# Retention and two feed-forwards: weight tiles asked for after the retention, conversion with four VectorE operations, a buffer of its own for x2

## The chip, the cores and the metric

The kernel runs on one core of a Trainium2 chip. The metric is the device time of one execution in microseconds, the median of three runs. All five engines are used: TensorE (PE, with its weight loads as PEld), VectorE (DVE), ScalarE (ACT), GpSimd (POOL) for a small multiplication, and SyncE (SP), whose queue issues nearly all DMA transfers.

## The reference

```python
# q, k, v: (4, 8, 576, 64); x then (2304, 512)
scores = matmul(q, k^T) / sqrt(64)
ret = scores * gamma_h ** (i - j)      # for i >= j, else 0
x = matmul(ret, v)                     # to 2304 tokens x 512
h = x @ w_in                           # 512 -> 2048
g = where(h >= 1, h, where(h <= -1, 0, (h + 1) ** 2 / 4))
x = g @ w_out                          # 2048 -> 512
out = ((x @ w_a) * (x @ w_b)) @ w_out2 # 512 -> 1536 -> 512
```

The weights are float64; the kernel gets them as raw 64-bit words.

## The kernel before

**Tiling.** The 2304 tokens are cut into 6 blocks of 384 (TB) and 18 chunks of 128. Every factor is held as two float32r parts, high and low, and a product is three matmuls (the list HL).

**Retention.** There are 36 units: a chunk times a half of the heads. A unit is loaded to `u` (L215), its values are scaled on POOL (L223), it is split into two parts `z` by ACT and DVE (L228, L229), its scores are formed on PE (`s`), masked and split (L245 to L251, `retf`, `ret`), and multiplied with the values and with the running state (`po`, `pn`). The product times the query factors, a part of the constant `con`, is the unit's share of x (L303: `xf`; L308 and L309 write both parts to `x`). The L309 rows therefore count finished units. The constant comes in two transfers on ACT's queue: a small one with masks and key factors, a large one (128 x 2560) with the query factors.

**Feed-forwards.** Work is cut in steps of one block of tokens and one chunk of 128 hidden columns. Five groups of steps follow each other: groups 0, 1 and 2 hold the hidden chunks 0 to 5, 6 to 10 and 11 to 15 of the first feed-forward, groups 3 and 4 the two halves of the second. In each group all six blocks are walked, so partial sums of groups 0 and 1 are stored to memory (`y`, L398) and read back in group 2 (`yin`, L390), where y_out adds them to x2, the second feed-forward's x, and stores it (x2d, L406). A step is l1 (12 matmuls `ph`, 24 in groups 3 and 4), an activation (L356 to L362, or L412 to L415) and l2 (12 matmuls `acc`, 9 wide ones later). The l2 of a step follows the l1 of the next.

**Retention beside group 0.** Six units, the first block's, run ahead; during each step of group 0 one more unit follows, until all 36 are done at the end of block 4.

**Weights.** A tile of weights is 128 x 512 words of 64 bits. It is loaded to `raw` (three buffers, L118) and converted to float32 by two ACT and four or five DVE operations (convert, L128 to L137: the float64's words are put together with shifts and masks, and L130 raises small magnitudes to a floor), then split into two parts (L142 on ACT, L143 on DVE) in one of 18 buffers, and of 14 more once the retention's buffers are gone. The main loop asks for tiles by a credit of one half per step, and at once where one of the next three steps needs one.

**Order.** The code's order gives priorities, and a scheduler with a plan of times puts the instructions of each engine in their final order: work that is asked for later fills holes in that plan. Every engine, and SP's queue, then works through its own list in order.

**x.** Blocks of x are stored once (xd) and loaded again for groups 1 and 2 (fetch_x, L340), asked for in the third step of the block before. x, and x2 in group 2, are taken from one pool of two buffers.

Of the kernel before, what the change touches and what calls it, by code (L numbers as in the profile page):

```python
# [9 lines left out]
F32 = mybir.dt.float32  # L10
F32R = mybir.dt.float32r
# [3 lines left out]
AF = mybir.ActivationFunctionType  # L15
ALU = mybir.AluOpType
# [3 lines left out]
P = 128  # L20
TB = 384
CPB = TB // P
GROUPS1 = [(0, 6), (6, 11), (11, 16)]
GROUPS2 = [(0, 6), (6, 12)]
WBUFS, WBUFS2 = 18, 14
MID = 288
UW = 1280
Q0, K0, R0, V0 = 0, 512, 768, 1024
# [46 lines left out]
def retention_ffn_kernel(  # L75
# [12 lines left out]
    nc = tc.nc  # L88
    B, H, S, D = shape
    DM = H * D  # L90
    NCC = DM // P
    NB = B * S // TB
# [4 lines left out]
    xpool = ctx.enter_context(tc.tile_pool(name="x", bufs=2))  # L97
# [8 lines left out]
    def mm(o, l, r, start, stop):  # L106
        nc.tensor.matmul(o, l, r, start=start, stop=stop)  # L107
# [8 lines left out]
    def load_raw(src):  # L116
        raw = rpool.tile([P, 512], I64, tag="raw", name="raw")
        nc.sync.dma_start(raw.rearrange("p (c f) -> p c f", f=src.shape[-1]), src)  # L118
        return raw

    def convert(raw):

        w = raw.bitcast(U32).rearrange("p (n t) -> p t n", t=2)
        low, high = w[:, 0, :], w[:, 1, :]
        r = raw.bitcast(I32).rearrange("p (n t) -> p t n", t=2)[:, 0, :]
        t = cpool.tile([P, 512], F32, tag="conv", name="conv")
        tu, ti = t.bitcast(U32), t.bitcast(I32)
        nc.scalar.activation(t, high.bitcast(F32), AF.Abs, scale=2.0 ** 16)  # L128
        nc.scalar.activation(r, low, AF.Copy, scale=2.0 ** -29)  # L129
        nc.vector.tensor_scalar(out=t, in0=t, scalar1=2.0, scalar2=None, op0=ALU.max)  # L130
        nc.vector.tensor_scalar(
            out=tu, in0=tu, scalar1=3, scalar2=None, op0=ALU.logical_shift_left
        )
        nc.vector.scalar_tensor_tensor(  # L134
            out=tu, in0=high, scalar=0x80000000, in1=tu, op0=ALU.bitwise_and, op1=ALU.bitwise_or
        )
        nc.vector.tensor_tensor(out=ti, in0=ti, in1=r, op=ALU.add)  # L137
        return t
# [23 lines left out]
    def fetch_to(n):  # L162
        while begun[0] < min(n, len(stream)):
            raws[begun[0]] = load_raw(stream[begun[0]][1])
            begun[0] += 1

    def weights_to(n):

        while made[0] < min(n, len(stream)):
            free = [r for r in room if room[r][1] > 0]  # L170
            if not free:
                return
            i = made[0]
            fetch_to(i + 1)
            key = stream[i][0]
            home[key] = free[0]
            room[free[0]][1] -= 1
            weights[key] = split(convert(raws.pop(i)), room[free[0]][0])
            made[0] += 1
            fetch_to(i + 3)  # L180

    def used(key):

        del weights[key]
        room[home.pop(key)][1] += 1
# [8 lines left out]
    con = apool.tile([P, const.shape[1]], F32, name="con")  # L194
# [3 lines left out]
    state = [apool.tile([P, 2 * P], F32, name=f"state{d}") for d in range(2)]  # L198
# [13 lines left out]
    def load_unit(u):  # L212
        if u < NU:
            units[u] = upool.tile([P, UW], F32, tag="u", name="u")
            nc.sync.dma_start(units[u], qkv[u // 2, u % 2])  # L215
# [96 lines left out]
    loaded, ready, scored, done = [0], [0], [0], [0]  # L312
# [25 lines left out]
    def fetch_x(b, space):  # L338
        t = xpool.tile([P, 2, NCC, TB], F32R, tag="x", name="x")
        nc.sync.dma_start(t.bitcast(F32), space[b])  # L340
        return t


    def l1(x, w):
        ph = ps.tile([P, 512], F32, tag="ps", name="ph")
        ops = []
        for cc in range(NCC):
            ws = slice(cc * P, (cc + 1) * P)
            for a, z in HL:
                ops.append((ph[:, :TB], w[:, a, ws], x[:, z, cc, :]))  # L350
        return ph, [(o, l, r, i == 0, i == len(ops) - 1) for i, (o, l, r) in enumerate(ops)]
# [34 lines left out]
    def fetch_y(b):  # L386
        for m in range(NCC):
            for i in range(2):
                t = yin[b, m, i] = ypool[0].tile([P, TB], F32, tag="yin", name="yin")
                nc.sync.dma_start(t, yd[i][b][:, m, :])  # L390

    def y_out(i, b):
        x = xpool.tile([P, 2, NCC, TB], F32R, tag="x", name="x2") if i == 2 else None
        for m, y in enumerate(ys.pop((i, b))):
            if i < 2:
                t = tpool.tile([P, TB], F32, tag="t", name="yst")
                (nc.scalar.copy if m % 2 else nc.vector.tensor_copy)(t, y[:, :TB])
                nc.sync.dma_start(yd[i][b][:, m, :], t)  # L398
            else:
                t, other = yin.pop((b, m, 0)), yin.pop((b, m, 1))  # L400
                nc.vector.tensor_add(t, t, other)
                nc.vector.tensor_add(t, y[:, :TB], t)
                nc.scalar.copy(x[:, 0, m, :], t)
                nc.vector.tensor_sub(x[:, 1, m, :], t, x[:, 0, m, :].bitcast(F32))
        if i == 2:
            nc.sync.dma_start(x2d[b], x.bitcast(F32))  # L406
# [44 lines left out]

    load_unit(0)
    cuts = [0, 2 * P + places * H, const.shape[1]]
    for i in range(2):
        nc.scalar.dma_start(con[:, cuts[i]:cuts[i + 1]], const[:, cuts[i]:cuts[i + 1]])
    load_unit(1)
    loaded[0] = 2
    fetch_to(1)

    warm = wpool.tile([P, 2, 512], F32R, tag="w", name="warm")  # L460
    nc.vector.memset(warm.bitcast(F32), 0.0)
    wacc = acc.tile([P, 512], F32, tag="acc0", name="wacc")
    for _ in range(8):
        mm(wacc, warm[:, 0, 0:P], warm[:, 1, :], True, True)
# [2 lines left out]
    for i in range(UPB):  # L467
        rounds_to(i + 1)
        weights_to(i)

    ypool = [None]
    gs = {}
    prev, back = None, None
    steps = [
        (i, b, f, f == f0, f == f1 - 1)
        for i, (f0, f1) in enumerate(GROUPS1 + GROUPS2) for b in range(NB) for f in range(f0, f1)
    ]

    def needed(step):
        return place[("o" if step[0] < 3 else "p", step[2])] + 1  # L480

    def finish(step):
        (l2 if step[0] < 3 else l2_2)(step)

    credit = 0.0
    for s, step in enumerate(steps):
        i, b, f, first, last = step
        f0, f1 = (GROUPS1 + GROUPS2)[i]
        credit += 0.5
        ahead = max(needed(t) for t in steps[s:s + 3])  # L490
        if made[0] < ahead:
            weights_to(ahead)
            credit = 0.0
        elif credit >= 1.0:
            weights_to(made[0] + 1)
            credit = 0.0
        if first:
            if i == 0:
                x = xt[b]
            else:  # L500
                x = xt.pop((i, b)) if (i, b) in xt else fetch_x(b, xd if i < 3 else x2d)
        due = min(UPB * (b + 1) + -(-(f - f0 + 1) * UPB // (f1 - f0)), NU) if i == 0 else NU
        if i < 3:
            ph, ops = l1(x, weights["i", f])
            for half in (ops[:6], ops[6:]):
                for o in half:
                    mm(*o)
                with tc.high_priority(60):
                    rounds_to(min(done[0] + 1, due))
            assert done[0] == due  # L510
            if b == NB - 1:
                used(("i", f))
            gs[step] = act1(ph)
        else:
            pair = []
            for j, key in enumerate("ab"):
                ph, ops = l1(x, weights[key, f])
                for o in ops:
                    mm(*o)
                pair.append(ph)  # L520
                if b == NB - 1:
                    used((key, f))
                if j == 0 and prev:
                    finish(prev)
                    prev = None
            gs[step] = act2(*pair)
        if prev:
            finish(prev)
        prev = step
        if i == 0 and first:  # L530
            nc.sync.dma_start(xd[b], x.bitcast(F32))
        if i == 0 and done[0] == NU and ypool[0] is None:
            att.close()
            ypool[0] = ctx.enter_context(tc.tile_pool(name="y", bufs=8))
            room["wx"] = [ctx.enter_context(tc.tile_pool(name="wx", bufs=WBUFS2)), WBUFS2]
        if i == 2 and first:
            fetch_y(b)
        if i == 4 and first:
            fetch_o(b)
        if f == f0 + 2:  # L540
            ni, nb = (i, b + 1) if b + 1 < NB else (i + 1, 0)
            if 0 < ni < 5 and not (ni == 0):
                xt[ni, nb] = fetch_x(nb, xd if ni < 3 else x2d)
# [25 lines left out]
```

## Time and profile before

| | us |
|---|---|
| median of 3 runs | 1026.21 (1025.89 to 1026.53) |
| the profiled execution | 1028.9 |
| its span | 1027.1 |
| PE busy / PEld busy | 984.7 / 942.3 |
| DVE / ACT / POOL busy | 585.7 / 438.2 / 32.0 |

The span goes from the first to the last instruction; the profiled execution's own time is a little longer. Matmuls are pipelined, so a busy PE need not be PE at its peak; PEld, the weight loads, stands beside it. The granted clock is a share of TensorE's full 2.4 GHz; 0.5 is its lower level of 1.2 GHz.

### The profile page before, as it was taken

How to read it: one execution, taken by the hardware profiler on the slowest of the kernel's cores; microseconds unless marked ns; L12 is line 12 of the kernel's file. 1: busy time of each engine (PE TensorE's matmuls, PEld its weight loads, DVE VectorE, ACT ScalarE, POOL GpSimd, SP SyncE). 2: the span in 40 equal slices, each digit the busy share in tenths (PEclk: the TensorE clock that was granted, in tenths of full speed). 3: DMA queues.
4: the chain of work that ended last, by engine and by line, in shares of the span. 5: the costliest groups of instructions: out<-in, count | busy, mean ns of one | idle time of the engine just before them, and what ended most of it. 6: DMA issues, size and time to landing. Idle time of an engine off the chain costs nothing.

```text
span 1027.1 us, 14058 instructions
## 1 busy us (share of the span) xinstructions
PE 984.7 (96%) x5504; PEld 942.3 (92%) x5504; DVE 585.7 (57%) x1083; ACT 438.2 (43%) x831; POOL 32.0 (3%) x44
## 2 busy tenths in 40 slices
PE   5699898999999999998999999999999999999998
PEld 4588797999999999998999999999999999999997
DVE  5999999788778933689456424534324321222222
ACT  5566665566567643676545323323222211111111
POOL 1111101110000000000000000000000000000000
PEclk6589899999999999999999999999999999999999
DMA  7564647255066852568665632532221131131100
GB/s 282 170 201 147 231 133 252 101 172 179 29 257 232 277 190 93 168 203 292 222 230 185 245 106 79 185 113 69 106 93 49 66 123 59 65 123 62 41 32 31
DMA packets 57475, 151.30 MB, mean 147 GB/s; under 512 B 4672, under 2 KB 37568, under 8 KB 52672
## 3 DMA queue, kind: packets, MB, share of 16 engines
q1 hardware_dynamic: 57120, 148.92, 41.6%
q10 hardware_dynamic: 288, 1.48, 0.4%
q8 instruction: 43, 0.70, 0.3%
q14 instruction: 24, 0.20, 0.1%
HBM read 112.63 MB, written 37.75 MB: 146 GB/s over the span
## 4 chain that ended last, share of the span: by engine, by line
PE 69%; DVE 16%; DMA 9%; issue 2%; ACT 2%; DVEq 0%; POOL 0%; SPq 0%; ACTq 0%
PE ph L107 40%; PE acc L107 25%; PE po L107 2%; DVE z L229 2%; DVE conv L134 2%; DVE conv L137 2%; DMA x<-xd 2%; DMA raw<-in_moe_w_in 2%; DMA y<-yst 1%; DMA raw<-in_moe_w_out 1%; DVE xf L303 1%; DVE t L358 1%; PE s L107 1%; DMA raw<-in_moe_w_b 1%; DVE w L143 1%
## 5 line engine op out<-in xcount | busy, mean ns | idle before, releaser
L107 PE MATMUL ph<-x,w 128*128 128x384 f32 x2880 | 535.4, 338 | 6.9 <-DMA x<-xd 3.9
L107 PEld LDWEIGHTS ph<-x,w 128*128 128x128 f32 x2880 | 507.7, 189 | 15.5 <-DMA x<-xd 4.6
L107 PE MATMUL acc<-g,w 128*128 128x384 f32 x1152 | 218.7, 336 | 1.5 <-ACT g L361 0.8
L107 PEld LDWEIGHTS acc<-g,w 128*128 128x128 f32 x1152 | 200.6, 188 | 2.8 <-ACT g L361 1.7
L413 DVE TENSOR_TENSOR t<-ph,t 128x384 f32<-128x384 f32 x72 | 40.1, 557 | 218.5 <-PE ph L107 214.6
L107 PE MATMUL acc<-w,g 128*128 128x512 f32 x648 | 161.5, 393 | 0.0
L107 PEld LDWEIGHTS acc<-w,g 128*128 128x128 f32 x648 | 120.5, 188 | 21.9
L414 ACT CAST g<-t 128x384 fp32r<-128x384 f32 x72 | 37.0, 514 | 187.1 <-DVE t L413 187.0
L412 ACT COPY t<-ph 128x384 f32<-128x384 f32 x72 | 34.5, 479 | 114.3 <-PE ph L107 114.3
L358 DVE SCALAR_TENSOR_TENSOR t<-t,ph 128x384 f32<-128x384 f32 x96 | 52.5, 550 | 38.7 <-ACT t L357 38.2
L356 ACT ACTIVATE t<-ph 128x384 f32<-128x384 f32 x96 | 47.0, 489 | 56.9 <-PE ph L107 51.6
L361 ACT CAST g<-t 128x384 fp32r<-128x384 f32 x96 | 49.1, 511 | 51.5 <-PE acc L107 27.3
L362 DVE TENSOR_TENSOR g<-t,g 128x384 fp32r<-128x384 f32 x96 | 53.2, 555 | 27.2 <-ACT g L361 27.0
L129 ACT ACTIVATE raw<-raw 128x512 int32<-128x512 uint32 x68 | 46.2, 679 | 46.5 <-DMA raw<-in_moe_w_out 15.6
L107 PE MATMUL s<-z 128*128 128x256 f32 x216 | 45.5, 324 | 18.6 <-ACT z L228 11.7
L229 DVE TENSOR_TENSOR z<-u,z 128x1280 fp32r<-128x1280 f32 x36 | 54.4, 1511 | 12.4 <-ACT z L228 12.2
L415 DVE TENSOR_TENSOR g<-t,g 128x384 fp32r<-128x384 f32 x72 | 40.1, 558 | 34.8 <-ACT g L414 34.8
L107 PEld LDWEIGHTS s<-z 128*128 128x128 f32 x216 | 35.3, 216 | 24.2 <-ACT z L228 15.4
L143 DVE TENSOR_TENSOR w<-conv,w 128x512 fp32r<-128x512 f32 x68 | 47.2, 694 | 17.3 <-ACT w L142 16.8
L107 PE MATMUL po<-ret,z 128*128 128x256 f32 x216 | 48.1, 319 | 7.4 <-ACT ret L250 5.2
L128 ACT ACTIVATE conv<-raw 128x512 f32<-128x512 f32 x68 | 45.7, 672 | 21.8 <-DVE w L143 10.8
L142 ACT CAST w<-conv 128x512 fp32r<-128x512 f32 x68 | 41.9, 616 | 26.9 <-DVE conv L137 26.8
(40 smaller groups left out, 721.9 us busy)
## 6 DMA issues: line engine op xcount, KB each, us to landing
u<-in_qkv SPq DMA_DIRECT2D x36, 640.0 KB, 4.1
x<-xd SPq DMA_DIRECT2D x12, 1536.0 KB, 6.9
x<-x2d SPq DMA_DIRECT2D x12, 1536.0 KB, 6.3
raw<-in_moe_w_out SPq DMA_DIRECT2D x28, 512.0 KB, 3.6
xd<-x SPq DMA_DIRECT2D x6, 1536.0 KB, 6.5
y<-yst SPq DMA_DIRECT2D x48, 192.0 KB, 3.7
yin<-y SPq DMA_DIRECT2D x48, 192.0 KB, 4.0
x2d<-x SPq DMA_DIRECT2D x6, 1536.0 KB, 6.4
```

What stands on the lines that cost most here:

```text
L107: nc.tensor.matmul(o, l, r, start=start, stop=stop)
L128: nc.scalar.activation(t, high.bitcast(F32), AF.Abs, scale=2.0 ** 16)
L129: nc.scalar.activation(r, low, AF.Copy, scale=2.0 ** -29)
L142: nc.scalar.copy(wt[:, 0, :], t)
L143: nc.vector.tensor_sub(wt[:, 1, :], t, wt[:, 0, :].bitcast(F32))
L229: nc.vector.tensor_sub(z[:, 1, :], t, z[:, 0, :].bitcast(F32))
L356: nc.scalar.activation(t, ph[:, :TB], AF.Relu, bias=0.5, scale=0.5)
L358: nc.vector.scalar_tensor_tensor(out=t, in0=t, scalar=1.0, in1=ph[:, :TB], op0=ALU.min, op1=ALU.max)
L361: nc.scalar.copy(g[:, 0, :], t)
L362: nc.vector.tensor_sub(g[:, 1, :], t, g[:, 0, :].bitcast(F32))
L413: nc.vector.tensor_mul(t, pb[:, :TB], t)
L415: nc.vector.tensor_sub(g[:, 1, :], t, g[:, 0, :].bitcast(F32))
```

## The change

Five edits. The conversion's L130 is dropped, and ACT's first operation scales by 2^-112 instead of 2^16, so that the floor isn't needed. While the retention runs beside group 0 (`busy`), the loop gives no credit for tiles and looks two steps ahead instead of three; in group 0's last block the credit is one tile per step. x2 gets a pool of its own with one buffer, and the second pool of weight tiles shrinks from 14 to 11. At the start the large part of the constant moves from ACT's queue to SP's, behind the third unit, which is now asked for at once. A small copy on ACT, of zeros, stands ahead of its first real work and takes the table load with it.

```diff
-WBUFS, WBUFS2 = 18, 14
+WBUFS, WBUFS2 = 18, 11
...
-        nc.scalar.activation(t, high.bitcast(F32), AF.Abs, scale=2.0 ** 16)
+        nc.scalar.activation(t, high.bitcast(F32), AF.Abs, scale=2.0 ** -112)
         nc.scalar.activation(r, low, AF.Copy, scale=2.0 ** -29)
-        nc.vector.tensor_scalar(out=t, in0=t, scalar1=2.0, scalar2=None, op0=ALU.max)
...
-        x = xpool.tile([P, 2, NCC, TB], F32R, tag="x", name="x2") if i == 2 else None
+        x = ypool[1].tile([P, 2, NCC, TB], F32R, tag="x2", name="x2") if i == 2 else None
...
-    for i in range(2):
-        nc.scalar.dma_start(con[:, cuts[i]:cuts[i + 1]], const[:, cuts[i]:cuts[i + 1]])
+    nc.scalar.dma_start(con[:, :cuts[1]], const[:, :cuts[1]])
     load_unit(1)
-    loaded[0] = 2
     fetch_to(1)
+    load_unit(2)
+    loaded[0] = 3
+    nc.sync.dma_start(con[:, cuts[1]:], const[:, cuts[1]:])
...
+    nc.scalar.copy(state[0][:, 0:8], warm[:, 0, 0:8].bitcast(F32))
...
-        credit += 0.5
-        ahead = max(needed(t) for t in steps[s:s + 3])
+        busy = i == 0 and b < NB - 1
+        credit += 0.0 if busy else 1.0 if i == 0 else 0.5
+        ahead = max(needed(t) for t in steps[s:s + 2 + (not busy)])
...
+            ypool[1] = ctx.enter_context(tc.tile_pool(name="x2", bufs=1))
```

The order of the instructions changes in three places that matter here. SP's queue at the very start, as the difference of the two orders:

```order
 L215 DMA u<-in_qkv 128x1280 x2
 L118 DMA raw<-in_moe_w_in 128x4x128
 L215 DMA u<-in_qkv 128x1280
+L459 DMA con<-in_const 128x2560
 L118 DMA raw<-in_moe_w_out 128x512
 L118 DMA raw<-in_moe_w_in 128x4x128
```

The first three units and the first weights are where they were; the large constant is new in this queue, ahead of the next weights. VectorE from the sixteenth finished unit on (an L309 row), in the kernel before:

```order
L309 TENSOR_TENSOR x<-xf,x 128x2x128
L358 SCALAR_TENSOR_TENSOR t<-t,ph 128x384
L143 TENSOR_TENSOR w<-conv,w 128x512
L130 TENSOR_SCALAR conv<-conv 128x512
L358 SCALAR_TENSOR_TENSOR t<-t,ph 128x384
L245 TENSOR_TENSOR retf<-s,con 128x512
L362 TENSOR_TENSOR g<-t,g 128x384
L131 TENSOR_SCALAR conv<-conv 128x512
L303 TENSOR_TENSOR xf<-po,con 64x256 x2
L130 TENSOR_SCALAR conv<-conv 128x512
L229 TENSOR_TENSOR z<-u,z 128x1280
L134 SCALAR_TENSOR_TENSOR conv<-raw,conv 128x512
```

and in the changed one, from its sixteenth L309:

```order
L309 TENSOR_TENSOR x<-xf,x 128x2x128
L245 TENSOR_TENSOR retf<-s,con 128x512
L362 TENSOR_TENSOR g<-t,g 128x384
L358 SCALAR_TENSOR_TENSOR t<-t,ph 128x384
L303 TENSOR_TENSOR xf<-po,con 64x256 x2
L251 TENSOR_TENSOR ret<-retf,ret 128x512
L229 TENSOR_TENSOR z<-u,z 128x1280
L362 TENSOR_TENSOR g<-t,g 128x384
L309 TENSOR_TENSOR x<-xf,x 128x2x128
L303 TENSOR_TENSOR xf<-po,con 64x256 x2
L229 TENSOR_TENSOR z<-u,z 128x1280
```

Before, conversions (`conv`, `w`) stand between the units here; in the changed order none does, since all of them that come before the retention's end stand further up. Ahead of these places the order before has 17 of each of L130, L131, L134, L137 and 16 of L143; the changed order has 20 of each of the first kinds that are left, and 18 of L143. SP's queue in group 2, with buffer numbers (xd2 is the third block's x, x2d0 the first block's x2), before:

```order
L390 DMA yin_5019<-y0_2_107 128x384
L390 DMA yin_5021<-y1_2_113 128x384
L406 DMA x2d0_99<-x2_4777 128x3072
L390 DMA yin_5023<-y0_2_107 128x384
L118 DMA raw_5663<-in_moe2_w_a 128x4x128
L340 DMA x_4891<-xd2_95 128x3072
```

and in the changed one:

```order
L340 DMA x_4844<-xd2_95 128x3072
L118 DMA raw_5310<-in_moe2_w_out 128x512
L118 DMA raw_5385<-in_moe2_w_a 128x4x128
L118 DMA raw_5498<-in_moe2_w_b 128x4x128
L118 DMA raw_5575<-in_moe2_w_out 128x512
L390 DMA yin_4763<-y1_1_112 128x384
L118 DMA raw_5684<-in_moe2_w_a 128x4x128
L390 DMA yin_4982<-y0_2_107 128x384
L390 DMA yin_4984<-y1_2_113 128x384
L406 DMA x2d0_99<-x2_4731 128x3072
```

The load of the third block's x has moved from behind the store of the first x2 to nine places ahead of it.

## Rows read from the trace of the kernel before

**Rows 1.** The page: busy time of TensorE, share of the span, instructions.
```profile
PE 984.7 (96%) x5504; PEld 942.3 (92%) x5504; DVE 585.7 (57%) x1083; ACT 438.2 (43%) x831; POOL 32.0 (3%) x44
```

**Rows 2.** Stretches: length, busy time of each engine, granted clock, DMA share, GB/s.
```profile
core 0: us, PE busy (x) PEld busy (x) DVE busy (x) ACT busy (x) POOL busy (x), PEclk, DMA share, GB/s
0.00:14.00 14.00, 6.32 (x16) 4.23 (x16) 4.09 (x4) 3.80 (x3) 2.05 (x7) 0.83 0.88 334
14.00:145.00 131.00, 111.75 (x626) 103.99 (x627) 127.00 (x233) 85.45 (x152) 16.40 (x20) 0.82 0.55 183
145.00:162.00 17.00, 15.30 (x99) 13.92 (x98) 16.82 (x33) 10.06 (x17) 1.27 (x2) 1.00 0.53 173
162.00:175.00 13.00, 10.27 (x51) 9.42 (x50) 10.97 (x21) 7.63 (x15) 1.91 (x2) 0.87 0.87 319
175.00:285.00 110.00, 110.00 (x755) 110.00 (x754) 90.90 (x159) 62.78 (x115) 10.41 (x15) 1.00 0.37 126
285.00:332.00 47.00, 46.75 (x270) 46.43 (x270) 38.76 (x77) 33.93 (x69) 0.00 (x0) 1.00 0.68 245
484.00:491.00 7.00, 6.63 (x22) 6.63 (x23) 4.59 (x10) 2.32 (x5) 0.00 (x0) 0.53 1.07 402
```

**Rows 3.** Lines of VectorE until 175 us: busy us, mean ns, idle before.
```profile
L134 DVE SCALAR_TENSOR_TENSOR conv<-raw,conv 128x512 uint32<-128x512 uint32 x20 | 14.6, 729 | 0.1
...
L137 DVE CUSTOM_DVE_ANT_0 conv<-raw,conv 128x1024 uint16<-128x1024 uint16 x20 | 14.1, 705 | 0.1
L143 DVE TENSOR_TENSOR w<-conv,w 128x512 fp32r<-128x512 f32 x18 | 12.7, 707 | 0.1
L130 DVE TENSOR_SCALAR conv<-conv 128x512 f32<-128x512 f32 x20 | 9.2, 463 | 0.6 <-ACT conv L128 0.5
L131 DVE TENSOR_SCALAR conv<-conv 128x512 uint32<-128x512 uint32 x20 | 8.3, 420 | 0.1
```

**Rows 4.** Line 309 until 147 us: count, duration, first and last start.
```profile
L309 DVE TENSOR_TENSOR x<-xf,x x16: 411/419/527, 22.6 to 146.1; 128x256 fp32r<-128x256 f32 x16
```

**Rows 5.** Timeline of the start: start us, duration us, instruction, idle before.
```profile
5.62 1.28 ACT L228 ACT_TABLE_LOAD   x1 [5.62 <-DMA u<-in_qkv]
5.79 0.61 POOL L223 TENSOR_TENSOR u<-u,con 128x256 f32<-128x256 f32 x1 [5.33 <-DMA con<-in_const]
6.91 1.26 ACT L228 CAST z<-u 128x1280 fp32r<-128x1280 f32 x1
...
10.38 0.61 POOL L223 TENSOR_TENSOR u<-u,con 128x256 f32<-128x256 f32 x1 [3.98 <-DMA u<-in_qkv]
...
12.31 1.49 DVE L229 TENSOR_TENSOR z<-u,z 128x1280 fp32r<-128x1280 f32 x1 [2.62 <-ACT z L228]
...
19.05 0.41 DVE L303 TENSOR_TENSOR xf<-po,con 64x256 f32<-64x256 f32 x1
```

**Rows 6.** DMA issues by line: count, KB each, median us to landing.
```profile
con<-in_const ACTq DMA_DIRECT2D x1, 1280.0 KB, 9.3
```

**Rows 7.** Timeline of PE in group 2.
```profile
473.37 7.21 PE L107 MATMUL acc<-g,w 128*128 128x384 f32 x40 [0.58 <-DVE g L362]
484.37 11.97 PE L107 MATMUL ph<-x,w 128*128 128x384 f32 x51 [3.79 <-DMA x<-xd]
496.18 2.24 PE L107 MATMUL acc<-g,w 128*128 128x384 f32 x12
498.26 0.51 PE L107 MATMUL ph<-x,w 128*128 128x384 f32 x2
```

**Rows 8.** Chain of waits in group 2: start us, us, what.
```profile
473.13 11.19 DMA x<-xd
```

**Rows 9.** The page: ACT's three operations of a conversion.
```profile
L129 ACT ACTIVATE raw<-raw 128x512 int32<-128x512 uint32 x68 | 46.2, 679 | 46.5 <-DMA raw<-in_moe_w_out 15.6
...
L128 ACT ACTIVATE conv<-raw 128x512 f32<-128x512 f32 x68 | 45.7, 672 | 21.8 <-DVE w L143 10.8
L142 ACT CAST w<-conv 128x512 fp32r<-128x512 f32 x68 | 41.9, 616 | 26.9 <-DVE conv L137 26.8
```

**Rows 10.** Waits: us in total, times, longest.
```profile
ACT raw L129 <- DMA raw<-in_moe_w_out: 15.6, 14, 2.8
```

More of the change, by code (lines that the diff above doesn't have):

```diff
@@ L469, in retention_ffn_kernel @@
         weights_to(i)
-    ypool = [None]
+    ypool = [None, None]
     gs = {}
```

## The prediction

> **What bounds the kernel now.** I read the page first. PE is busy for 96% of the span and PEld (its weight loads) for 92% [rows 1], so the question is where TensorE waits, and no other engine's total matters. Then the table by stretches [rows 2]. It shows three regimes. Until 14 us everything waits for the first loads. From 14 to 162 us VectorE is the bound: DVE is busy for 127.0 of 131 and 16.82 of 17 us, while PEld has 103.99 and 13.92. In this time each unit of the retention and the weight tiles of the first group share VectorE. From 175 to 285 us PE and PEld are busy for all 110 us at clock 1.00, with DVE at 90.90: TensorE is the bound, and stays it to the end. So an operation taken off VectorE counts before about 170 us only. Third, the timeline of PE and the chain of waits show one hole in the later stages: at 484.37 us a matmul has waited 3.79 us for the load of x from xd [rows 7], which the chain shows as one transfer of 11.19 us issued at 473.13 [rows 8].
>
> **Part A, the start.** The first loads are reordered: the 1280 KB of query factors leave ScalarE's queue and follow the third unit on SP's. Now the second unit's load lands when POOL starts on it, at 10.38 us, after 3.98 us of idle time, and VectorE's split of that unit starts at 12.31 [rows 5]. The big constant was on the wires for 9.3 us in the same time [rows 6]. The stretch moves 334 GB/s [rows 2]. Without the constant ahead of it, the second unit (128 x 1280 x 4 bytes, 655 kB) needs 2.0 us after the first, which lets the table load start at 5.62; so it lands at 7.6, and POOL (0.61) and ACT (1.26) bring VectorE's split to 9.5: 2.8 us earlier. The constant now lands behind 524 + 655 + 1311 kB more, 7.5 us later, at 15.1. Its first user, L303, stood at 19.05 and would stand at 16.3, later still because one conversion is moved ahead of it in the order; so 1.2 us cover it. The early table load takes 1.28 us off ACT's first cast at 6.91, but POOL ends at 6.40 anyway, and the second unit decides. I take A = -2.8. Bounds: -3.98 (POOL's whole wait), and +2.1, if the loads run at the 183 GB/s of the next stretch: the constant then lands at 21.2, 2.1 us behind L303's present place.
> The Trainium skill, "DMA: Bandwidth & Descriptors", section "Issuing engines are not separate DMA queues", speaks against it: loads from all queues run on the same 16 DMA engines and interleave, and spreading them only saves issue time. The row of the constant agrees that they share. By the page alone moving a load between queues gains nothing and A would be 0, the sum 2.8 us less; I hold that order within one queue changes who is served first.
>
> **Part B, VectorE until 175 us.** The maximum (L130) goes: 20 of them in this time at 463 ns, 9.2 us [rows 3]. But the order moves something too. The code asks for weights later; the built order has them earlier, because conversions fill holes in the planned VectorE time. Before the sixteenth L309 (at 146.1 us, [rows 4]) stand 17 first halves of a conversion in the kernel before; in the changed one 20, all there are before the retention ends. Three more first halves (L131, L134, L137: 420 + 729 + 705 ns) are 5.6 us and two more L143 at 707 ns 1.4, together 7.0; 17 maxima less are 7.9. So up to that place VectorE's work is the same within 1 us: nothing is gained there beyond A, and I count 0. After it VectorE has no conversions left, where the kernel before has three first halves and two L143 to do, and TensorE can take over as the bound at once. What can be gained is therefore what TensorE loses from 145 to 175 us. PEld is busy for 13.92 of 17 and 9.42 of 13 us, so 6.7 us are lost; and a granted clock of 0.87 in the last 13 us means half speed (1.2 of 2.4 GHz) for 26% of them, 3.4 us, which cost 1.7. That is 8.4. With conversions gone VectorE's load falls to about that of the stretch from 175 us on (90.90 of 110), where TensorE loses nothing, but two engines so close in load cost something at the takeover: I leave 1.8, about the half-speed part. B = -6.6. Bounds: -9.2, all 20 maxima, and +4.0: VectorE has less to do, so it can lose by waits only, and its idle time from 14 to 145 us (131 - 127.0) may double where conversions stand earlier.
> Here PE's own row would say less: 15.30 of 17 and 10.27 of 13 us, a loss of 4.4. [...] By the matmul row B would be 2.3 us less. The trace sides with the weight loads: 98 and 50 loads in 30 us against 754 in the next 110.
> The other 48 maxima fall where TensorE is the bound, and count nothing; TensorE's full rows from 175 to 285 us are the cover. Without cover they would be 48 x 435 ns = 21 us.
>
> **Part C, x of the second feed-forward.** x and x2 share two buffers. In group 2 the loaded x, the running x and x2 need three places, so the load of the next x is issued only when the last l1 of the running block has let go: at 473.13, with 40 matmuls of other work left to cover it. With a buffer for x2 alone, the load of block b+1 takes the place of block b-1 and has a block (about 21 us of matmuls) to land its 11.19. The order agrees: xd2 now stands ahead of x2d0's store, and stood behind it. What goes: 3.79 us of idle time, and what follows it. From 484.37 to 496.18 us 51 matmuls take 11.81 us; twelve of the same width take 2.08 right behind (496.18 to 498.26, [rows 7]), so 51 should take 8.84; the granted clock was 0.53 meanwhile [rows 2]. That is 2.97 more. C = -6.8. Bounds: 0 (another wait stands behind it; a loss is excluded, since the load has more time in every block) and -7.4 (with the 0.58 us of waiting in the same block, [rows 7]). x2 in one buffer must be stored before the next block writes it, a block later: nothing. WBUFS2 from 14 to 11 leaves 29 weight tiles; groups 2 and 3 need 10 + 18, so none is missing.
>
> **Sum.** -2.8 - 6.6 - 6.8 = -16.2 us. The profiled execution took 1028.9 us (span 1027.1), 2.7 above the median of 1026.21; its own time would be 1012.7, and the median 1010.0.
>
> **Rivals.**
> 1. VectorE is no longer in TensorE's way at any time before 175 us, and the start gains all of POOL's wait: A = -4.0, B = -9.2, C = -7.4, -20.6 or 1005.6. For it: DVE idles for 4 of 131 us only, so any work removed shows. Against: before the sixteenth L309 the order adds as much as it removes. 17%.
> 2. The VectorE gain is lost (B between 0 and +4.0, conversions moved early delay the units): 1016.6 to 1020.6. For it: that same order, and VectorE holds the chain until 162 us. 17%.
> 3. The hole in group 2 moves rather than goes, because SP works its queue in order and the load of x stands among stores and y loads that wait: C = 0, 1016.8. Against: a block of slack. 8%.
> 4. The change doesn't do what it says: weights come no later but earlier, and with dearer waits at the start (A = +2.1, B = +4.0, C = -6.8): 1025.5, no change. 3%.
> 5. Slower. The conversions pushed behind the retention stand in ACT's and DVE's queues ahead of activations. In the last block of group 0 and the first of group 1 the order has 13 conversions in 11 steps now, and had 11. ACT is busy 33.93 of 47 us there [rows 2]; two more of 672 + 679 + 616 ns [rows 9] make 37.9. If each of the 13 waits for its load the 2.8 us that is the longest now [rows 10], 36.4 us, ACT is 27.3 us over the 47: 1010.0 + 27.3 = 1037.3. It decides from 9.1 us of such waits on, 0.7 each, and makes the kernel slower than before from 25 us on. Against: 14 such waits total 15.6 us in the whole run. 4%.
>
> **How the numbers follow.** Forecast 1010.0, 51%. The range runs from 1004 (rival 1 and a little) to 1019 (rivals 2 and 3 and the bounds of each part); it leaves out rivals 4 and 5 and the far tails, 15 to 20%. All cases but 4 and 5 are faster; 0.2%, 2.1 us, is about what can be told from no change. Faster 0.92, same 0.03, slower 0.05.
>
> **What the changed profile would show.** A: POOL's second multiplication near 7.6 us, and L303 not waiting for the constant. B: no row of L130; PEld full from about 150 us instead of 175, and all that follows 9 us earlier. C: no wait of ph for x from xd, clock 1.00 through group 2. Wrong if PEld still loses 6 us in the 30 us after the sixteenth L309, if a wait for raw or x of more than 3 us stands on PE, or if L303 waits for con.

## The result, and the profile after

The changed kernel takes 1007.8 us (median of four runs, 1007.49 to 1008.12) against 1026.26 (1025.89 to 1026.53, also four runs): a ratio of 0.982, 95% interval 0.9803 to 0.9837, 18.5 us. The same pair on another chip gave 0.980 (0.9777 to 0.9824). The forecast was 1010.0, -16.2 us. One execution among all the runs of this document, of the kernel with 15 + 14 tiles below, took 2147.03 us; it counts in that run's median and not in its ratio. The profiled execution took 1007.49 us with a span of 1005.7; the one of before, 1028.9, lay 2.6 above its median, so differences between the two traces can be up to some 3 us larger than those of the medians.

Stretches of the changed kernel, with the columns of [rows 2]:

```profile
0.00:14.00 14.00, 8.56 (x27) 6.73 (x27) 7.64 (x10) 6.99 (x9) 2.28 (x7) 0.81 0.88 335
14.00:145.00 131.00, 110.31 (x649) 102.05 (x649) 128.36 (x230) 89.84 (x160) 17.14 (x20) 0.86 0.60 202
145.00:162.00 17.00, 16.68 (x113) 16.25 (x112) 15.74 (x28) 11.10 (x20) 1.51 (x3) 1.00 0.75 257
162.00:175.00 13.00, 13.00 (x91) 13.00 (x91) 11.51 (x20) 7.02 (x14) 1.61 (x2) 1.00 0.36 121
...
420.00:530.00 110.00, 110.00 (x636) 110.00 (x635) 75.56 (x148) 64.63 (x131) 0.00 (x0) 1.00 0.75 266
```

From 14 to 145 us VectorE is as full as before. From 145 to 175 us PEld is busy for 29.25 of 30 us, where [rows 2] had 13.92 + 9.42, and the clock is full: TensorE takes over as the bound at about 145 us instead of 175. From 420 to 530 us, around group 2, it is full: the hole of [rows 7] is gone. The same stretch of the kernel before:

```profile
420.00:530.00 110.00, 105.62 (x592) 104.99 (x591) 81.57 (x163) 66.97 (x134) 0.00 (x0) 0.97 0.67 230
```

SP's queue shows why, with the loads of x in that time (start us, duration us, engine, line):

```profile
437.14 0.34 SPq L340 DMA_DIRECT2D x<-xd  x1
458.54 1.20 SPq L340 DMA_DIRECT2D x<-xd  x1
484.83 0.42 SPq L340 DMA_DIRECT2D x<-xd  x1
503.70 0.32 SPq L340 DMA_DIRECT2D x<-xd  x1
```

They are issued about a block of work apart, each a block ahead of its use. In the trace's list of waits, x from xd no longer stands against PE.

The start of the changed kernel, the rows that answer to [rows 5]:

```profile
5.33 0.61 POOL L223 TENSOR_TENSOR u<-u,con 128x256 f32<-128x256 f32 x1 [4.88 <-DMA con<-in_const]
5.98 1.26 ACT L228 CAST z<-u 128x1280 fp32r<-128x1280 f32 x1 [3.31 <-POOL u L223]
6.78 0.61 POOL L223 TENSOR_TENSOR u<-u,con 128x256 f32<-128x256 f32 x1 [0.83 <-DMA u<-in_qkv]
7.27 2.94 DVE L229 TENSOR_TENSOR z<-u,z 128x1280 fp32r<-128x1280 f32 x2 [5.33 <-ACT z L228]
...
15.77 0.85 DVE L303 TENSOR_TENSOR xf<-po,con 64x256 f32<-64x256 f32 x2
```

POOL has the second unit at 6.78 us instead of 10.38, VectorE splits both units without a break, and L303 runs at 15.77 with no wait for the large constant. The count of finished units (L309: count, shortest, median and longest ns, first and last start in us), of the kernel before and of the changed one:

```profile
L309 DVE TENSOR_TENSOR x<-xf,x x36: 410/419/835, 22.6 to 285.3; 128x256 fp32r<-128x256 f32 x36
```

```profile
L309 DVE TENSOR_TENSOR x<-xf,x x16: 409/417/420, 20.6 to 142.4; 128x256 fp32r<-128x256 f32 x16
L309 DVE TENSOR_TENSOR x<-xf,x x36: 409/418/839, 20.6 to 272.6; 128x256 fp32r<-128x256 f32 x36
```

The sixteenth unit is 3.7 us earlier than in [rows 4] (142.4 against 146.1), the last one 12.7 (272.6 against 285.3). So 3.7 us come before the sixteenth unit and 9.0 behind it.

### The profile page after: what moved, and what is told of

Its sections match the earlier page's. It is cut to its first block, busy times and chain, and to the rows that moved or that the text cites. A ratio compares the mean times of both kernels' runs of the same rounds, so it can differ in the third digit from the quotient of the medians.

```text
span 1005.7 us, 14000 instructions
## 1 busy us (share of the span) xinstructions
PE 973.4 (97%) x5504; PEld 933.3 (93%) x5504; DVE 563.7 (56%) x1015; ACT 438.6 (44%) x832; POOL 32.6 (3%) x44
## 4 chain that ended last, share of the span: by engine, by line
PE 81%; DVE 10%; DMA 4%; ACT 2%; issue 2%; DVEq 0%; POOL 0%; SPq 0%; ACTq 0%
PE ph L107 45%; PE acc L107 31%; PE po L107 3%; DVE z L229 2%; PE s L107 1%; DVE w L143 1%; DVE conv L137 1%; DVE conv L134 1%; PE pn L107 1%; DVE xf L303 1%; DMA raw<-in_moe_w_b 1%; DMA raw<-in_moe_w_out 1%; DMA y<-yst 1%; DVE ret L251 1%; DVE retf L245 1%
## 5 line engine op out<-in xcount | busy, mean ns | idle before, releaser
L358 DVE SCALAR_TENSOR_TENSOR t<-t,ph 128x384 f32<-128x384 f32 x96 | 52.3, 550 | 30.6 <-ACT t L357 30.1
L130 ACT ACTIVATE raw<-raw 128x512 int32<-128x512 uint32 x68 | 46.1, 679 | 45.6 <-DMA raw<-in_moe_w_b 13.1
L107 PE MATMUL s<-z 128*128 128x256 f32 x216 | 43.4, 315 | 15.2 <-ACT z L228 10.3
L229 DVE TENSOR_TENSOR z<-u,z 128x1280 fp32r<-128x1280 f32 x36 | 54.3, 1510 | 6.7 <-ACT z L228 6.5
L143 DVE TENSOR_TENSOR w<-conv,w 128x512 fp32r<-128x512 f32 x68 | 47.2, 694 | 18.8 <-ACT w L142 18.3
L142 ACT CAST w<-conv 128x512 fp32r<-128x512 f32 x68 | 41.9, 616 | 22.5 <-DVE conv L137 22.5
```

The costliest lines, as they stand in the source:

```text
L142: nc.scalar.copy(wt[:, 0, :], t)
L143: nc.vector.tensor_sub(wt[:, 1, :], t, wt[:, 0, :].bitcast(F32))
L229: nc.vector.tensor_sub(z[:, 1, :], t, z[:, 0, :].bitcast(F32))
L358: nc.vector.scalar_tensor_tensor(out=t, in0=t, scalar=1.0, in1=ph[:, :TB], op0=ALU.min, op1=ALU.max)
```

## The experiments

All times are ratios to the kernel before, run on the same chip beside them; its median was 1027 to 1029 us on these chips. The last two columns are starts in the one trace of each run: of the sixteenth finished unit and of the last one (L309; its line number is one lower or higher in some runs). They are 146.1 and 285.3 us in the kernel before, 142.4 and 272.6 in the changed one.

| run | median us | ratio | 95% interval | sixteenth unit us | last unit us |
|---|---|---|---|---|---|
| no L130 alone | 1022.12 | 0.9951 | 0.9934 to 0.9969 | 145.8 | 279.9 |
| start alone | 1029.67 | 1.0011 | 0.9994 to 1.0027 | 145.7 | 286.0 |
| x2's buffer alone | 1019.46 | 0.9925 | 0.9901 to 0.995 | 145.7 | 284.1 |
| credit alone | 1025.84 | 0.9981 | 0.9965 to 0.9997 | 145.3 | 285.8 |
| changed, old start | 1014.17 | 0.987 | 0.9849 to 0.9891 | 145.2 | 279.6 |
| changed, with L130 | 1020.69 | 0.9933 | 0.9914 to 0.9953 | 144.8 | 284.7 |
| changed, old credit | 1009.08 | 0.9819 | 0.9795 to 0.9842 | 143.5 | 273.7 |
| changed, 12 + 17 tiles | 1007.41 | 0.9805 | 0.9781 to 0.983 | 132.7 | 268.6 |
| changed, again | 1007.97 | 0.98 | 0.9777 to 0.9824 | 142.7 | 273.0 |
| changed, 15 + 14 tiles | 1009.48 | 0.9819 | 0.9789 to 0.9848 | 138.0 | 272.9 |
| changed, 18 L143 on POOL | 1017.54 | 0.9891 | 0.9867 to 0.9916 | 147.2 | 281.7 |
| start alone, four raw buffers | 1024.05 | 0.9964 | 0.9943 to 0.9986 | 142.6 | 280.1 |

**One part alone.** The edits are those of the diff above, one part at a time, in the kernel before.

No L130:

> The kernel before with one edit: no L130, and the scale that makes it unnecessary. Theory (the gain at the retention comes from VectorE's time alone): the built order has all 20 first halves of conversions before the sixteenth finished unit, as in the changed kernel, so B shows here in full, -6.6 to -9 us: 1017 to 1020, the last L309 7 to 9 us earlier than 285.7 us, and the hole in group 2 stays. Rival 1 (the later credit is what frees the units): under -3 us, 1023 to 1026. Rival 2 (TensorE is the bound there anyway): 0, 1026.

It gave 0.9951, 5.0 us (3 to 7 by its interval): less than the 6.6 to 9 of the theory, whose low end the interval just reaches, and more than rival 1 allows. The last unit is 5.4 us earlier, not 7 to 9. The order is as the theory had it: in this run's trace VectorE does 20 first halves ahead of the sixteenth unit and none between it and the last. So the order alone does not bring B in full. The start's edits:

> The kernel before with the start's edits alone: large constant on SP behind the third unit, third unit asked for at once, table load ahead. Theory: A = -2.8 to -4, which VectorE, busy from then on, carries to the end: 1022 to 1023.5; POOL's second multiplication near 6.8 us. Rival (the slack is eaten by later waits of the units, as loads cost the same in sum): 0, 1026.

The rival came true: no change. The rows below, of this run's SP, DVE and ACT between 18 and 35 us, show where VectorE waits again:

```profile
18.45 7.22 SPq L215 DMA_DIRECT2D u<-in_qkv  x2
27.22 0.38 SPq L118 DMA_DIRECT2D raw<-in_moe_w_in  x1
...
26.51 0.68 DVE L137 CUSTOM_DVE_ANT_0 conv<-raw,conv 128x1024 uint16<-128x1024 uint16 x1
...
33.66 0.43 DVE L130 TENSOR_SCALAR conv<-conv 128x512 f32<-128x512 f32 x1 [1.42 <-ACT conv L128]
34.80 1.49 DVE L229 TENSOR_TENSOR z<-u,z 128x1280 fp32r<-128x1280 f32 x1 [0.72 <-ACT z L228]
...
32.43 0.66 ACT L129 ACTIVATE raw<-raw 128x512 int32<-128x512 uint32 x1 [2.44 <-DMA raw<-in_moe_w_in]
```

A conversion's last reader of raw, L137, ends at 27.19 (26.51 + 0.68). SP has waited for it, and issues the next load of weights at 27.22. ACT waits for it 2.44 us, the next unit's cast queues behind that, and VectorE waits 1.42 and 0.72 us for ACT. The last run below has one raw buffer more. Then x2's buffer and the credit:

> The kernel before with a buffer of its own for x2 and 11 instead of 14 weight tiles in the second pool. Theory: C = -6.8 to -7.7, 1018.5 to 1019.5, no wait of PE for x from xd and no half clock in group 2. Rival (the load of x waits elsewhere in SP's queue, or the three tiles fewer cost something): 1023 to 1027.

> The kernel before with the later credit alone (busy, two steps ahead, one tile per step in block 5). Theory: nothing, since the built order of every engine is that of the kernel before until the retention ends; only the tiles of group 1 come in another order: 1025.2 to 1027.2, all 18 tiles made before the eighteenth unit ends. Rival (the edit does what it says): six tiles of conversion, 15 us of VectorE, leave the retention's time: 1015 to 1020.

x2's buffer gave 0.9925, 7.7 us, as the theory had it. The credit gave 0.9981, 1.9 us with an interval that ends just short of 1; nothing of the 15 us of its rival. What the 1.9 us would be, if they are there, is open.

**One part undone,** in the changed kernel:

> The changed kernel with the old start (large constant on ACT's queue, third unit not asked for early). Alone the start's edits gave nothing: VectorE's 4 us were given back as waits in units 3 to 8. Theory (the start pays only where the order behind it has no such waits, as in the changed kernel, whose idle VectorE time stays at 7 to 8 us): 3 to 5 us slower than the changed kernel, 1011 to 1013, ratio to before 0.985 to 0.987. Rival (the start is worth nothing here either): 1007 to 1009, 0.982.

> The changed kernel with L130 put back. Theory (VectorE's time, and with it the order, carries the retention's gain): conversions are spread to the eighteenth unit again and B goes: 8 to 11 us slower than the changed kernel, 1016 to 1019, ratio 0.990 to 0.993. Rival (each part adds by itself, the maximum being worth the 5.0 us that its removal alone gave): 1012 to 1013, 0.987.

> The changed kernel with the old credit. Theory: the order until the retention's end is the same; 0 to 2 us slower than the changed kernel, 1007 to 1010, ratio 0.981 to 0.984. Rival (the credit matters): 1012 and more.

All three went as the theory said, two with a little more loss than it gave: 0.987 (1014.17 us where 1011 to 1013 was expected), 0.9933 (1020.69 where 1016 to 1019 was) and 0.9819. Against 0.982, and against the median of 1007.97 on the same chip, the changed kernel loses 5 to 6 us without its start and 12 to 13 without the shorter conversion; without the credit it loses nothing that can be told (0 to 1). One stretch tells these kernels apart, 145 to 175 us; here for no L130 alone, the changed kernel with the old start, the start alone, and the changed kernel with L130:

```profile
145.00:175.00 30.00, 27.40 (x186) 26.99 (x185) 24.92 (x45) 17.39 (x32) 3.14 (x5) 1.00 0.58 202
```

```profile
145.00:175.00 30.00, 27.16 (x183) 26.76 (x182) 26.02 (x46) 18.43 (x33) 3.48 (x5) 1.00 0.56 196
```

```profile
145.00:175.00 30.00, 24.61 (x136) 22.56 (x135) 29.53 (x53) 17.32 (x32) 2.58 (x4) 0.89 0.67 236
```

```profile
145.00:175.00 30.00, 24.95 (x134) 22.49 (x133) 28.62 (x51) 16.80 (x31) 3.42 (x4) 0.89 0.68 238
```

With L130 PEld is busy for 22.5 us of 30 with the new start, and for 23.3 without it ([rows 2], 13.92 + 9.42), and VectorE is nearly full. Without L130 it is 26.8 to 27.0, and 29.25 where the new start stands beside that, in the changed kernel.

**Weights that are really late.** The credit doesn't delay tiles 13 to 18; fewer places do:

```diff
-WBUFS, WBUFS2 = 18, 11
+WBUFS, WBUFS2 = 12, 17
```

> The changed kernel with 12 and 17 instead of 18 and 11 weight tiles in the two pools: now tiles 13 to 18 have no place before the retention ends, and the weights of group 1 are really made later. Before the sixteenth unit VectorE has six first halves and six L143 less, 15 us. Theory (VectorE bounds TensorE until the last early conversion): most of what TensorE still loses from 75 to 175 us goes (11 us by its start-to-start times): 6 to 9 us faster than the changed kernel, 999 to 1002, ratio 0.973 to 0.976. Rival (the six tiles come back as waits in the last block of group 0 and in group 1, where conversions stand ahead of activations): 1006 to 1012.

It gave 0.9805, no different from the changed kernel: the rival. The sixteenth unit is 9.7 us earlier than in the changed kernel and the last one 4.0, and in the end nothing is left. Two stretches, first of this run, then of the changed kernel:

```profile
100.00:150.00 50.00, 49.43 (x331) 48.52 (x330) 41.85 (x73) 28.23 (x51) 7.25 (x7) 1.00 0.47 158
275.00:325.00 50.00, 45.79 (x252) 44.82 (x251) 41.31 (x78) 37.58 (x76) 0.00 (x0) 0.97 0.68 229
```

```profile
100.00:150.00 50.00, 46.03 (x298) 43.42 (x297) 48.49 (x88) 34.59 (x62) 4.23 (x6) 1.00 0.60 204
275.00:325.00 50.00, 49.21 (x284) 48.89 (x283) 41.87 (x79) 38.80 (x78) 0.00 (x0) 1.00 0.72 247
```

PEld is busy for 5.1 us more from 100 to 150 us (3.4 more than in the second trace of the changed kernel), and for 4.1 less from 275 to 325, at a clock of 0.97. There TensorE waits 3.5 us for L358, an activation, where the changed kernel waits 0.8; VectorE waits 5.2 us for ACT's half of conversions (1.3 in the changed kernel), and ACT 8.0 us for loads of weights (5.5). That the six tiles' conversions stand ahead of activations there is the reading that fits these waits. The middle way (`15, 14`):

> The changed kernel with 15 and 14 weight tiles: three tiles, not six, wait for the retention's end. With six, TensorE lost 4.8 us less from 100 to 150 us and 6 us more from 275 to 325. Theory (both effects go by the tile, the loss only once conversions crowd the last block of group 0): most of the gain, a third of the loss, 1 to 3 us faster than the changed kernel, ratio 0.979 to 0.981. Rival (what is moved is paid back whole): 0.982 to 0.984.

0.9819 against 0.98 of the changed kernel beside it, whose expectation was

> The changed kernel as it is, for a direct comparison on this chip. 0.982 of the kernel before, 0.980 to 0.984.

None of its runs, 1009.12 us and more, is as fast as the slowest of the changed kernel's six beside it (1006.95 to 1008.6). So the rival is right that nothing is gained. The trace has the loss elsewhere than in group 1: the sixteenth unit is 4.4 us earlier (138.0 against 142.4), and the last one already is not (272.9 against 272.6).

**VectorE's work on another engine.**

```diff
-        nc.vector.tensor_sub(wt[:, 1, :], t, wt[:, 0, :].bitcast(F32))
+        eng = nc.gpsimd if made[0] < 18 else nc.vector
+        eng.tensor_sub(wt[:, 1, :], t, wt[:, 0, :].bitcast(F32))
```

> The changed kernel with the low part's subtraction (L143) of the first 18 tiles on POOL instead of VectorE. VectorE has 18 x 0.69 = 12.5 us less before the sixteenth unit; nothing else moves off its list. Theory (VectorE's time bounds TensorE until 150 us): 5 to 9 us faster than the changed kernel, ratio 0.973 to 0.977, the sixteenth L309 8 us earlier than 142.8. Rival (POOL's operation, some 1.7 us by its 857 ns for half the size, holds up VectorE's or the units' multiplications): no gain or a loss, 0.982 to 0.990.

0.9891, 9.6 us slower than the changed kernel beside it. The sixteenth unit is 4.8 us later than in the changed kernel, not 8 earlier. Lines of VectorE from 14 to 145 us in this run (columns as in [rows 3]; its lines are numbered one higher from 143 on), and of the changed kernel:

```profile
L134 DVE SCALAR_TENSOR_TENSOR conv<-raw,conv 128x512 uint32<-128x512 uint32 x19 | 16.2, 852 | 0.2
...
L131 DVE TENSOR_SCALAR conv<-conv 128x512 uint32<-128x512 uint32 x19 | 11.3, 592 | 1.3 <-ACT conv L129 1.3
...
L296 DVE TENSOR_TENSOR st<-state,st 128x256 fp32r<-128x256 f32 x15 | 8.5, 567 | 0.5 <-ACT st L295 0.5
...
L363 DVE TENSOR_TENSOR g<-t,g 128x384 fp32r<-128x384 f32 x10 | 7.1, 715 | 0.6 <-ACT g L362 0.6
```

```profile
L134 DVE SCALAR_TENSOR_TENSOR conv<-raw,conv 128x512 uint32<-128x512 uint32 x19 | 14.3, 752 | 0.1
...
L131 DVE TENSOR_SCALAR conv<-conv 128x512 uint32<-128x512 uint32 x19 | 8.1, 427 | 0.1
L295 DVE TENSOR_TENSOR st<-state,st 128x256 fp32r<-128x256 f32 x16 | 7.0, 439 | 0.1
...
L362 DVE TENSOR_TENSOR g<-t,g 128x384 fp32r<-128x384 f32 x11 | 6.1, 550 | 0.8 <-ACT g L361 0.8
```

On the mean of this stretch these lines take 13 to 30% longer, and the shift L131 39%; others that also read two operands in the on-chip memory gain little (z, L229 in the changed kernel: 3%) or nothing (ret, L251). The mean hides what happens. L131 from 14 to 145 us, first with POOL's subtractions, then in the changed kernel (count, shortest, median and longest ns):

```profile
L131 DVE TENSOR_SCALAR conv<-conv x19: 410/415/1518, 16.9 to 116.9; 128x512 uint32<-128x512 uint32 x19
```

```profile
L131 DVE TENSOR_SCALAR conv<-conv x19: 411/419/574, 16.6 to 135.4; 128x512 uint32<-128x512 uint32 x19
```

The median has not moved: single operations are held up, by up to 1.1 us. In the timeline the 12 of the 19 that overlap no operation of POOL take 0.41 to 0.43 us, and the seven that overlap one 0.41 to 1.52. POOL's subtraction takes 1493 ns, where VectorE's takes 707 [rows 3]; whether the operations held up or the later tiles cost more was not separated.

**The start, with a fourth raw buffer.**

```diff
-WBUFS, WBUFS2 = 18, 14
+WBUFS, WBUFS2 = 18, 13
...
-    rpool = ctx.enter_context(tc.tile_pool(name="raw", bufs=3))
+    rpool = ctx.enter_context(tc.tile_pool(name="raw", bufs=4))
```

> The start's edits alone, as in the run that gave nothing, with four raw buffers instead of three (and 13 instead of 14 tiles in the second pool to make room): a load of weights waits for a conversion one further back, and stands between the units' loads in SP's queue. Theory (the start's 4 us were given back because the load issued at 27 us waited for a raw buffer, and ACT and VectorE then waited behind it): VectorE's idle time stays near 7 us until unit 8 instead of 12, and 2 to 4 us of the gain show: 1024 to 1026 where the kernel before has 1028, ratio 0.996 to 0.998. Rival (other waits of the units take its place, or VectorE, bound in any case, has its work ordered no better): 0.9995 to 1.002, idle time 11 to 13 us at unit 8.

0.9964, 3.7 us (1.4 to 5.9 by its interval): the size that the theory gave. The stretch from 24 to 80 us, of the start alone and with four buffers:

```profile
24.00:80.00 56.00, 43.06 (x221) 40.70 (x221) 50.58 (x92) 32.70 (x56) 6.04 (x8) 0.82 0.54 179
```

```profile
24.00:80.00 56.00, 44.17 (x246) 41.20 (x247) 55.42 (x101) 37.16 (x65) 6.53 (x9) 0.79 0.57 186
```

VectorE idles 5.4 us of 56 with three buffers and 0.6 with four. The built order changed with the buffer: from 25 us on, loads of weights and of units alternate in SP's queue, much as in the changed kernel; the start alone, with three buffers, has two units in a row there. ACT still waits for raw, 1.58 us at 34.07, but VectorE no longer waits behind it. Four buffers in the kernel before, with its old start, weren't run, so what the fourth buffer is worth by itself is open.

## Why the prediction was right, and which terms were off

**What bounds it.** The three regimes held in the changed kernel: VectorE until the last early conversion, TensorE from there on. The hole in group 2 is gone.

**Part A, forecast -2.8.** Its mechanism held where it was put: POOL at 6.78 us (forecast 7.6), L303 at 15.77 (16.3), the constant in time. The sixteenth unit came 3.7 us earlier, and 2.8 of them are the start's: with the old start in the changed kernel it stood at 145.2. What failed is that the sum carries A to the end whatever stands behind: alone the start is worth nothing. With the shorter conversion it is worth 5.1 us (0.987 against 0.982), and by the last unit 7.0 (279.6 against 272.6), 4.2 of them behind the sixteenth.

What gave the gain back alone is, by the trace, a wait for a raw buffer. With a fourth buffer VectorE's waits are gone and 3.7 us show, but the order changed with it, so the buffer is the likely cause and not shown apart. That the shorter conversions avoid the wait in the changed kernel is read from its trace, where VectorE waits once, for 0.6 us, between 26 and 82 us; which place in the order does it was not isolated.

The rule of the Trainium skill, "DMA: Bandwidth & Descriptors", section "Issuing engines are not separate DMA queues", that loads share the same engines from whichever queue they come, does not explain the missing gain: the second unit did land 3.6 us earlier. The constant's large part was issued at 3.00 us, behind the loads of three units and one of weights, where before it was issued by 1.64 us, beside the second unit's; whether the queue or the later place did it was not run apart.

**Part B, forecast -6.6.** Before the sixteenth unit the order did what the text read from it: without the new start it came 0.3 to 0.9 us earlier. Behind it 9.0 us came. From the sixteenth unit to the last, before and after:

```profile
146.10:285.30 139.20, 134.77 (x896) 132.54 (x895) 117.58 (x209) 79.80 (x144) 13.59 (x18) 0.99 0.44 151
```

```profile
142.40:272.60 130.20, 129.88 (x888) 129.45 (x887) 110.95 (x194) 77.03 (x138) 13.53 (x18) 1.00 0.44 150
```

PEld lost 6.66 us of 139.20 before and 0.75 of 130.20 after: 5.9. The half clock is the forecast's 1.7. Eight weight loads fewer are left to do there (887 against 895), at 0.146 us each (110.00 us for 754, [rows 2]) 1.2. Together that is 8.8. The mis-sized term is thus the 1.8 us left for the takeover, of which 0.75 came.

The forecast has no term for the start's part in this. Without the new start all 20 first halves stand ahead of the sixteenth unit too, and none between it and the last. Yet PEld loses 3.0 to 3.2 us from 145 to 175 us (no L130 alone, and the changed kernel with the old start), where TensorE waits for z and ret, and only 4.8 to 5.1 us come behind the sixteenth unit, not 9.0. So conversions out of the way did not let TensorE take over at once, as the text has it; the new start was needed as well. What it changes in the order there was not isolated.

By PE's own busy time the loss goes from 4.43 to 0.32 us in these two rows, 4.1 where the weight loads have 5.9; with 4.1 the terms would reach 7.0 of the 9.0. The Trainium skill's "Perfetto Trace Analysis", section "Identifying the Most-Contended Engine", holds that matmul busy time is no good measure of the distance to the roofline and names the busy share of weight loads as one to use; this trace agrees.

B was also priced as one of three terms that add. With x2's buffer it does: no L130 (5.0) and x2's buffer (7.7) make 12.7, and the changed kernel with the old start, which has both and the credit, 13.4. With the start it doesn't: no L130 gives 5.0 us alone and 11.6 in the changed kernel, the start nothing alone and 5.1 there.

**Part C, forecast -6.8.** 7.7 alone (5 to 10 by its interval; the forecast's bound was 7.4), the hole and its half clock gone: from 420 to 530 us this run has PEld at 109.51 of 110 and a clock of 1.00.

**The credit,** counted at nothing, is nothing that can be told in the changed kernel (0.9819 against 0.982). The weights are not made later by it: with it alone VectorE still does 17 first halves until 147 us, as before. Where they are made later, by fewer places, nothing is won.

**Sum.** -16.2 against -18.5. In the traces A and B together gave 12.7 where 9.4 was forecast, and C alone gave 7.7 where 6.8 was. Their 20.4 is more than the 18.5 of the medians by 1.9, inside the 3 us by which the traces can differ more. The total is near in part by luck: the retention's 9.4 is a sum that doesn't hold, since its two parts are worth 0 and 5.0 us alone, and that together they bring 12.7 was not foreseen. Of the rivals, 1 (1005.6) came near in its size for the retention; 2 to 5 did not occur. The wait of rival 5, conversions ahead of activations, did show, at 4 us, when six more tiles were pushed there.

## What to carry to other kernels

Where one engine is full, removing an operation is worth its time only if the next engine can take the stretch over: read where the built order puts the rest, not where the code asks for it, and price the edit together with the others that touch the same stretch. Here one edit was worth nothing alone and 5 us beside another, and the other 5 alone and 12 beside the first; a test of each part alone would have dropped the start. A transfer that comes earlier paid only where the waits behind it were gone too. Work moved out of the full stretch (six tiles) brought 4 us there and cost as much where it landed.

## What the runs showed of the hardware

In the run with POOL's subtractions, single operations of VectorE that overlap one of POOL's were held up: L131 took up to 1518 ns, while its median stayed (415 against 419 ns) and its mean rose by 39%. A hole of 3.79 us on TensorE cost 7.7 us, about twice its length (x2's buffer alone, which takes it away): the granted clock was 0.53 in the 7 us from 484 us on ([rows 2, 7]), and the 51 matmuls there took 2.97 us more than at the rate of the twelve behind them. In the changed kernel the clock is 1.00 in every stretch shown from 145 us on.
